# Summing the output in four column groups of TensorE instead of two, and emptying them with two copies per engine

## The chip, the cores and the metric

The kernel runs on one core of a Trainium2 chip. The metric is the device time of one execution in microseconds (us). A profile is one execution taken by the hardware profiler; its span (209.9 us for the kernel before) leaves out about 1.7 us that the timed run has (211.66 us for the same execution).

Three engines matter here: TensorE (PE in the profile, its weight loads are PEld), VectorE (DVE) and ScalarE (ACT). SPq is the queue that issues the transfers. PSUM is the memory in which TensorE's sums are kept; its rows are called partitions, and a sum lies in one of its banks. A column group is named here by the partition at which an output starts: 0, 32, 64 or 96. The granted clock (PEclk) is the share of its full speed at which TensorE runs.

## The reference, cut to what matters

One decode step of attention plus an MLP, added:

```
xn  = layernorm(x)                       # 4 x 576
A   = attention(xn, k_cache, v_cache)    # 32 heads, 16 KV heads, the last 2048 keys
A   = A.reshape(4, 4096) @ wo            # 4 x 576
B   = x1 + gelu(layernorm(x1) @ w3) @ w4 # x1 = xn + hs; one token, so hs = 0 and x1 = xn
out = x + A + B                          # 4 x 576, bfloat16
```

Some 87 MB of keys, values and weights are read for an output of 4.5 KB.

## The kernel before

All transfers are queued in one order: wq, keys and values by head, w3 and wo between them, and w4 last, in six pieces of 18, 6, 6, 4, 1 and 1 terms. A term is 128 rows of wo or w4 times 576 columns. Every term of both products, and x + xn, is added into one sum in PSUM, which is emptied at the very end.

```python
NI = 2; CW = D // NI            # two halves of 288 columns
OR = NI * B                     # 8 output rows: one for each (batch, half)
OW = OR + NI                    # weights of 4 columns, spread and padded with zeros,
ROWS = slice(NI - 1, NI - 1 + OR, NI)
gT = cleared([P, NF, OW], "gT") # so that each half lands in its own 4 of the 8 rows
op = cleared([P, WOR, OW], "op")
acc = ps_acc.tile([P, CW], F32)
nc.vector.memset(acc[:], 0.0)

def acc_matmuls(terms):         # two terms per call; late in the kernel the odd one
    for i in range(NI):         # goes to acc_odd, in another column group and bank
        for n, (lhsT, rhs) in enumerate(terms):
            to, q, start = (second[0], QD, second[1]) if second and n % 2 else (acc, 0, False)
            nc.tensor.matmul(out=to[q:q + OR, :], lhsT=lhsT[:, NI - 1 - i:NI - 1 - i + OR],
                             rhs=rhs[:, i * CW:(i + 1) * CW], start=start, stop=False, ...)
...
W4_PIECES = [0, NFH, NF - 12, NF - 6, NF - 2, NF - 1, NF]      # NF = 36
...
mlp_out(*pieces[0]); ...; mlp_out(*pieces[3])   # even terms to acc, odd terms to acc_odd
second.clear()                                  # the last two terms go to acc alone
odd = const.tile([OR, CW], F32)
nc.scalar.activation(out=odd[:], in_=acc_odd[QD:QD + OR, :], func=ACT.Copy)
seen = const.tile([1, 1], F32)
nc.vector.tensor_copy(out=seen[:], in_=odd[0:1, 0:1])
for lo, hi in pieces[4:]:
    mlp_out(lo, hi)
fin = const.tile([OR, CW], out.dtype)
nc.vector.tensor_tensor(out=fin[:], in0=acc[0:OR, :], in1=odd[:], op=ALU.add)
nc.sync.dma_start(out=o2.rearrange("b (i n) -> (b i) n", i=NI), in_=fin[:])
```

## Time and profile before

| | kernel before |
|---|---|
| median time | 211.47 us (3 runs), 211.49 us (4 runs) |
| span of the profile | 209.9 us |
| share of the span of the queue that loads | 97.5% of 16 engines |
| last w4 bytes moving | until about 206.45 us |
| store issued | 207.78 us |

The page of the kernel before: the granted TensorE clock and the DMA share in tenths, over 40 equal slices of the span, and then the line of the loading queue (packets, MB, share of the 16 engines' span).

```profile
PEclk9999769999996557976999999999997968899969
DMA  8999999999999999999999999999999999999991
...
q1 hardware_dynamic: 6640, 87.17, 97.5%
```

The transfer engines are full from the second slice to the last but one (the page has 415 GB/s read over the span). So the kernel is bound by its loads, and a change in the sum can only win in what comes after the last load. The timeline of the kernel before, at its end, shows that part (start in us, duration, engine, line, operation, output<-inputs, shape, count, and in brackets how long the engine had been idle and what ended that):

```profile
200.70 0.40 PE L183 MATMUL acc<-w_sb,gT 128*8 128x288 bf16 x1 [0.78 <-DMA w_sb<-in_B_w_dram]
200.70 0.40 PE L183 MATMUL acc_odd<-w_sb,gT 128*8 128x288 bf16 x1
200.89 0.44 PE L183 MATMUL acc<-w_sb,gT 128*8 128x288 bf16 x1
...
204.13 0.29 PE L183 MATMUL acc<-w_sb,gT 128*8 128x288 bf16 x1
...
204.25 0.29 PE L183 MATMUL acc<-w_sb,gT 128*8 128x288 bf16 x1
...
206.12 0.28 PE L183 MATMUL acc<-w_sb,gT 128*8 128x288 bf16 x1
...
206.60 0.65 PE L183 MATMUL acc<-w_sb,gT 128*8 128x288 bf16 x4
206.81 0.40 ACT L612 ACTIVATE odd<-acc_odd 8x288 f32<-8x288 f32 x1 [10.46 <-PE acc_odd L183]
207.25 0.14 DVE L614 COPY seen<-odd 1x1 f32<-1x1 f32 x1 [8.54 <-ACT odd L612]
207.32 0.43 DVE L619 TENSOR_TENSOR fin<-acc,odd 8x288 bf16<-8x288 f32 x1
207.78 0.37 SPq L620 DMA_DIRECT2D out_dram<-fin  x1
```

The two matmuls of a pair run side by side, and a pair is the work of one term. Pairs follow each other every 0.24 us at first (the granted clock is 0.50) and every 0.12 us from about 204 us on (clock 1.00). At 206.12 the piece of four terms starts; the four matmuls at 206.60 are the two last terms, one after the other in one group. The copy of acc_odd is nearly hidden behind them. Then come the add (0.43) and the store. The windows of the same stretch (busy time of each engine with its count, granted clock, DMA share, GB/s) show where the last bytes are:

```profile
206.40:206.50 0.10, 0.10 (x7) 0.07 (x3) 0.00 (x0) 0.00 (x0) 0.00 (x0) 1.00 0.08 23
206.50:206.60 0.10, 0.10 (x6) 0.07 (x1) 0.00 (x0) 0.00 (x0) 0.00 (x0) 1.00 0.00 0
```

### The profile page before, as it was taken

To read this page: it belongs to the slowest core of one execution; us is meant where nothing else is said; L and a number is where in the kernel's file an instruction comes from. 1 tells how busy PE (TensorE), PEld (TensorE's weight loads), DVE (VectorE), ACT (ScalarE), POOL (GpSimd) and SP (SyncE) were. 2 spreads that over 40 slices of the span, in tenths; PEclk is the share of its full clock that TensorE was granted. 3 is DMA by queue.
4 is the path that set the end of the run, shared out by engine and by line. 5 is a ranking of instruction groups with operands and counts; after the bars stand their busy time and mean duration, and the time that the engine had idled before them with its cause. 6 is when DMAs were issued, how large, how long until landed. Compare 5 with 4: busy or idle time off the path is not lost.

```text
span 209.9 us, 2326 instructions
## 1 busy us (share of the span) xinstructions
PE 149.1 (71%) x941; PEld 60.2 (29%) x955; DVE 113.7 (54%) x165; ACT 34.4 (16%) x66; POOL 8.9 (4%) x33
## 2 busy tenths in 40 slices
PE   0378198699670039649998999659995976898684
PEld 0123032233220013223454333224331312343353
DVE  3611877985910084917507898465949391755200
ACT  7612201021120001111120312110111111113100
POOL 4620000000000000000000300000000000000000
PEclk9999769999996557976999999999997968899969
DMA  8999999999999999999999999999999999999991
GB/s 294 406 403 440 422 428 431 437 425 432 448 429 419 421 437 421 447 418 437 434 425 437 418 426 439 434 423 440 418 431 437 422 433 431 434 428 446 417 399 71
DMA packets 6658, 87.31 MB, mean 416 GB/s; under 512 B 748, under 2 KB 1016, under 8 KB 1656
## 3 DMA queue, kind: packets, MB, share of 16 engines
q1 hardware_dynamic: 6640, 87.17, 97.5%
q8 instruction: 7, 0.11, 0.2%
q10 hardware_dynamic: 8, 0.00, 0.0%
q14 instruction: 3, 0.02, 0.0%
HBM read 87.17 MB, written 0.00 MB: 415 GB/s over the span
## 4 chain that ended last, share of the span: by engine, by line
DMA 52%; PE 24%; DVE 19%; issue 2%; ACT 1%; SPq 0%; DVEq 0%; ACTq 0%
DMA vn<-in_A_v_cache_dram 19%; DMA w_sb<-in_B_w_dram 15%; DVE kt L226 14%; DMA kn<-in_A_k_cache_dram 12%; PE S L342 9%; DMA wq_sb<-in_A_wq_dram 6%; PE acc L183 4%; PE O L394 2%; PE g_ps L460 2%; PE q_ps L286 2%; DVE mx L348 2%; PE S L364 1%; PE oT L407 1%; DVE PT L376 1%; DVE dm L350 1%
## 5 line engine op out<-in xcount | busy, mean ns | idle before, releaser
L342 PE MATMUL S<-kt,qz 128*128 128x512 bf16 x242 | 74.0, 429 | 34.5 <-DVE kt L226 31.3
L226 DVE STREAM_TRANSPOSE kt<-kn 128x2048 int32<-128x2048 int32 x32 | 73.4, 2295 | 26.5 <-DMA kn<-in_A_k_cache_dram 25.0
L342 PEld LDWEIGHTS <-qz 128*128 128x128 bf16 x256 | 24.0, 108 | 63.5 <-issue 46.6
L394 PE MATMUL O<-vn,PT 128*32 128x512 bf16 x256 | 22.9, 400 | 8.4 <-DMA vn<-in_A_v_cache_dram 8.4
L370 ACT ACTIVATE E<-S 128x512 bf16<-128x512 f32 x16 | 9.5, 597 | 97.7 <-PE S L364 97.7
L376 DVE STREAM_TRANSPOSE PT<-E 128x512 bf16<-128x512 bf16 x16 | 11.4, 710 | 15.5 <-ACT E L370 15.5
L401 ACT ACTIVATE O_sb<-O,rd 128x512 f32<-128x512 f32 x16 | 11.0, 686 | 37.1 <-PE O L394 37.1
L394 PEld LDWEIGHTS <-PT 128*32 128x32 bf16 x256 | 5.9, 94 | 29.6 <-issue 28.6
L417 DVE TENSOR_REDUCE on<-oT 128x8 bf16<-128x128 f32 x16 | 4.6, 287 | 16.7 <-PE oT L407 16.6
L348 DVE TENSOR_REDUCE mx<-S 128x1 f32<-128x512 f32 x16 | 10.5, 658 | 1.2 <-PE S L342 1.1
L407 PE MATMUL oT<-ident_w,O_sb 128*128 128x128 f32 x64 | 11.0, 296 | 0.3 <-ACT O_sb L401 0.3
L407 PEld LDWEIGHTS oT<-ident_w,O_sb 128*128 128x128 f32 x64 | 7.0, 146 | 4.6 <-issue 3.9
L183 PE MATMUL acc<-wo_sb,op 128*8 128x288 bf16 x56 | 7.5, 286 | 1.0 <-DVE op L439 1.0
L364 PE MATMUL S<-nm,j_row 8*128 8x512 bf16 x16 | 6.3, 393 | 1.9 <-DVE nm L360 1.7
L183 PE MATMUL acc<-w_sb,gT 128*8 128x288 bf16 x38 | 6.6, 342 | 0.8 <-DMA w_sb<-in_B_w_dram 0.8
L380 PE MATMUL dn<-rs,same_j 128*128 128x1 f32 x32 | 6.4, 268 | 0.0
L380 PEld LDWEIGHTS dn<-rs,same_j 128*128 128x128 f32 x32 | 5.2, 204 | 4.1 <-issue 3.4
L330 PE MATMUL S<-negbig,ohT 4*128 4x512 bf16 x16 | 6.1, 384 | 0.0
L183 PE MATMUL acc_odd<-w_sb,gT 128*8 128x288 bf16 x34 | 6.1, 350 | 0.0
L183 PEld LDWEIGHTS <-op 128*8 128x8 bf16 x64 | 4.6, 87 | 3.2 <-DVE op L439 1.1
L286 PE MATMUL q_ps<-wq_sb,xnT 128*32 128x512 bf16 x40 | 4.5, 630 | 1.3 <-DMA wq_sb<-in_A_wq_dram 1.3
L478 DVE COPY g_x<-gT_ps 128x64 f32<-128x64 f32 (+1 forms) x3 | 0.6, 194 | 8.5 <-PE gT_ps L472 8.5
(93 smaller groups left out, 80.7 us busy)
## 6 DMA issues: line engine op xcount, KB each, us to landing
kn<-in_A_k_cache_dram SPq DMA_DIRECT2D x16, 2048.0 KB, 23.8
vn<-in_A_v_cache_dram SPq DMA_DIRECT2D x16, 2048.0 KB, 25.6
wo_sb<-in_A_wo_dram SPq DMA_DIRECT2D x4, 1152.0 KB, 26.4
w_sb<-in_B_w_dram SPq DMA_DIRECT2D x1, 4608.0 KB, 33.2
wq_sb<-in_A_wq_dram SPq DMA_DIRECT2D x1, 4096.0 KB, 12.8
w_sb<-in_B_w_dram SPq DMA_DIRECT2D x1, 2592.0 KB, 32.2
w_sb<-in_B_w_dram SPq DMA_DIRECT2D x2, 864.0 KB, 34.0
w_sb<-in_B_w_dram SPq DMA_DIRECT2D x2, 576.0 KB, 32.5
```

What stands on the lines that cost most here:

```text
L183: nc.tensor.matmul(out=to[q:q + OR, :], lhsT=lhsT[:, NI - 1 - i:NI - 1 - i + OR], rhs=rhs[:, i * CW:(i + 1) * CW], start=start, stop=False ...
L226: nc.vector.transpose(out=kt[:], in_=src)
L286: nc.tensor.matmul(out=q_ps[r][g * QD:(g + 1) * QD, :], lhsT=xnT[:, k, :], rhs=wq_sb[:, col:col + NW], start=(j == 0), stop=False, skip_gr ...
L342: nc.tensor.matmul(out=S_ps[h][:], lhsT=qz[:, z0:z0 + P], rhs=kt[:, ib, c0:c0 + SC, e:2 * QD:2].rearrange("p c k -> p (c k)"), start=False ...
L348: nc.vector.reduce_max(out=mx[:], in_=S_ps[h][:], axis=AX.X)
L364: nc.tensor.matmul(out=S_ps[h][:], lhsT=j_row[:], rhs=st.pop(("nm", h))[:, 0:1].to_broadcast([NJ, NW]), start=False, stop=False, skip_grou ...
L370: nc.scalar.activation(out=E[h][:].rearrange("p c k -> p (c k)"), in_=S_ps.pop(h)[:], func=ACT.Exp, scale=scale, accum_out=rs[:])
L376: nc.vector.transpose(out=PT[h][:], in_=E.pop(h)[:])
L380: nc.tensor.matmul(out=dn[:], lhsT=same_j[:], rhs=st.pop(("rs", h))[:], start=True, stop=True)
L394: nc.tensor.matmul(out=O_ps[h][g * QD:(g + 1) * QD], lhsT=PT[h][:, c, :], rhs=vn[:, :, c, :], start=(s == 0), stop=False, skip_group_check ...
L401: nc.scalar.activation(out=O_sb[h][:], in_=O_ps.pop(h)[:], func=ACT.Copy, scale=st.pop(("rd", h))[:, 0:1])
L407: nc.tensor.transpose(out=oT[:, s, :], in_=o[:, s, :], identity=ident_w[:, s * NJ:s * NJ + P])
```

## The change

The intent: use all four column groups, so that a term takes half the streaming time; need no zero-padded weights, no second sum and no add; and empty the four quarters with two engines at once.

```diff
-    NI = 2
+    NI = 4
@@ weights and sums
-    gT = cleared([P, NF, OW], "gT")
-    op = cleared([P, WOR, OW], "op")
-    acc = ps_acc.tile([P, CW], F32)
-    nc.vector.memset(acc[:], 0.0)
+    gT = const.tile([P, NF, B], BF16, name="gT")
+    op = const.tile([P, WOR, B], BF16, name="op")
+    accs = [ps_acc.tile([P, CW], F32, name=f"acc{i}") for i in range(2)]
+    for acc in accs:
+        nc.vector.memset(acc[:], 0.0)
+    def acc_of(i):
+        return accs[i * 2 // NI][i * QD:i * QD + B, :]
@@ acc_matmuls (old body cut)
+        for lhsT, rhs in terms:
+            for i in range(NI):
+                nc.tensor.matmul(out=acc_of(i), lhsT=lhsT, rhs=rhs[:, i * CW:(i + 1) * CW],
+                                 start=False, stop=False, skip_group_check=True)
@@ mlp_g: the hidden layer gives up its own bank
-        g_ps = ps_acc.tile([P, P, n], F32, tag="g", name="g_ps")
+        g_ps = (ps_o if r < 2 else ps_m).tile([P, P, n], F32, tag="O" if r < 2 else "m", name="g_ps")
@@ the end (acc_odd, odd and seen are cut)
-    nc.vector.tensor_tensor(out=fin[:], in0=acc[0:OR, :], in1=odd[:], op=ALU.add)
-    nc.sync.dma_start(out=o2.rearrange("b (i n) -> (b i) n", i=NI), in_=fin[:])
+    fin = const.tile([B, D], out.dtype)
+    for i in range(NI):
+        dst = fin[:, i * CW:(i + 1) * CW]
+        if i * 2 < NI:
+            nc.vector.tensor_copy(out=dst, in_=acc_of(i))
+        else:
+            nc.scalar.activation(out=dst, in_=acc_of(i), func=ACT.Copy)
+    nc.sync.dma_start(out=o2, in_=fin[:])
```

Quarters 0 and 1 lie in one bank at partitions 0 and 32, quarters 2 and 3 in the other at 64 and 96. VectorE empties the first bank, ScalarE the second.

More of the change, by code (lines that the diff above doesn't have):

```diff
@@ L166 @@
     qz = cleared([P, ZP + Hkv * 4 * P], "qz")
-    OR = NI * B
-    OW = OR + NI
-    ROWS = slice(NI - 1, NI - 1 + OR, NI)
-    gT = cleared([P, NF, OW], "gT")
-    op = cleared([P, WOR, OW], "op")
-    acc = ps_acc.tile([P, CW], F32)
-    nc.vector.memset(acc[:], 0.0)
-    second = []
-    def acc_matmuls(terms):
-        for i in range(NI):
-            for n, (lhsT, rhs) in enumerate(terms):
-                to, q, start = (second[0], QD, second[1]) if second and n % 2 else (acc, 0, False)
-                nc.tensor.matmul(out=to[q:q + OR, :], lhsT=lhsT[:, NI - 1 - i:NI - 1 - i + OR],
-                                 rhs=rhs[:, i * CW:(i + 1) * CW], start=start, stop=False, skip_group_check=True)
-                if start:
-                    second[1] = False
+    gT = const.tile([P, NF, B], BF16, name="gT")
[5 more added lines that the diff above has]
+        return accs[i * 2 // NI][i * QD:i * QD + B, :]
+    def acc_matmuls(terms):
+        for lhsT, rhs in terms:
+            for i in range(NI):
+                nc.tensor.matmul(out=acc_of(i), lhsT=lhsT, rhs=rhs[:, i * CW:(i + 1) * CW],
+                                 start=False, stop=False, skip_group_check=True)
     def layernorm(dst_f, dst_bf, src):
@@ L268 @@
     nc.vector.reduce_sum(out=own[:], in_=ident_f[:].rearrange("p (h d) -> p h d", h=WOH), axis=AX.X)
-    idz = const.tile([B, OW], F32)
-    nc.gpsimd.memset(idz[:], 0.0)
-    nc.gpsimd.tensor_copy(out=idz[:, ROWS], in_=ident_f[0:B, 0:B])
     xsum = xn_f
     nc.gpsimd.tensor_tensor(out=xsum[:], in0=xn_f[:], in1=x_bf[:], op=ALU.add)
-    acc_matmuls([(idz[:], xsum)])
+    acc_matmuls([(ident_f[0:B, 0:B], xsum)])
     ln2_bf = part(D, B)
@@ L438, in o_pick @@
         with nc.allow_low_precision("one term is not zero"):
-            nc.vector.reduce_sum(out=op[:, :, ROWS], in_=mk[:].rearrange("p i h b -> p i b h"), axis=AX.X)
+            nc.vector.reduce_sum(out=op[:], in_=mk[:].rearrange("p i h b -> p i b h"), axis=AX.X)
     def o_proj(h):
@@ L443, in o_proj @@
             return
-        for i in range(0, WOR, 2):
-            acc_matmuls([(op[:, i + u, :], wo_tiles[h // WOQ][:, i + u, :]) for u in range(2)])
+        acc_matmuls([(op[:, i, :], wo_tiles[h // WOQ][:, i, :]) for i in range(WOR)])
     G_CHUNKS = [(e, 4 * g, 4) for e in range(2) for g in range(NQD)] + [(e, 16, 2) for e in range(2)]
@@ L486, in mlp_act @@
         nc.gpsimd.tensor_scalar(out=u[:], in0=u[:], scalar1=0.5, scalar2=0.5, op0=ALU.mult, op1=ALU.add)
-        nc.gpsimd.tensor_tensor(out=gT[:, :, ROWS], in0=u[:], in1=xs[:], op=ALU.mult)
+        nc.gpsimd.tensor_tensor(out=gT[:], in0=u[:], in1=xs[:], op=ALU.mult)
     def mlp_out(lo, hi):
         w4 = w_tiles["w4"]
-        for i in range(lo, hi, 2):
-            acc_matmuls([(gT[:, u, :], w4[:, u, :]) for u in range(i, min(i + 2, hi))])
+        acc_matmuls([(gT[:, u, :], w4[:, u, :]) for u in range(lo, hi)])
     order = [("K", 0), ("K", 1), ("K", 2)]
@@ L598 @@
     pieces = list(zip(W4_PIECES, W4_PIECES[1:]))
-    acc_odd = ps_acc.tile([P, CW], F32, tag="g", name="acc_odd")
-    second += [acc_odd, True]
     o_turn(hl)
@@ L605 @@
     o_proj(hl)
-    mlp_out(*pieces[0])
-    mlp_out(*pieces[1])
-    mlp_out(*pieces[2])
-    mlp_out(*pieces[3])
-    second.clear()
-    odd = const.tile([OR, CW], F32)
-    nc.scalar.activation(out=odd[:], in_=acc_odd[QD:QD + OR, :], func=ACT.Copy)
-    seen = const.tile([1, 1], F32)
-    nc.vector.tensor_copy(out=seen[:], in_=odd[0:1, 0:1])
-    for lo, hi in pieces[4:]:
-        mlp_out(lo, hi)
-    fin = const.tile([OR, CW], out.dtype)
-    nc.vector.tensor_tensor(out=fin[:], in0=acc[0:OR, :], in1=odd[:], op=ALU.add)
-    nc.sync.dma_start(out=o2.rearrange("b (i n) -> (b i) n", i=NI), in_=fin[:])
+    for lo, hi in pieces:
+        mlp_out(lo, hi)
+    fin = const.tile([B, D], out.dtype)
[6 more added lines that the diff above has]
+    nc.sync.dma_start(out=o2, in_=fin[:])
 _INS = ['A_x', 'A_k_cache', 'A_v_cache', 'A_wq', 'A_wo', 'B_x', 'B_w1', 'B_w2', 'B_w3', 'B_w4']
```

## The prediction

> What bounds it now. The transfers. The 40-slice rows show DMA at 9 or more in every slice but the first and last, and the queue table gives the loading queue 97.5% of the span; in the chain of waits DMA holds 52%. Windows of the end: the last w4 bytes move until about 206.45 us of the 209.9 us span. So the change can only win in what lies after that, 3.45 us, of which the store (issue at 207.78 to the end) is 2.1.
>
> The end before (timeline, chain): the first half of w4 lands at 200.65; then matmul pairs (acc and acc_odd, 288 columns, side by side, one pair is one term's work) run one every 0.24 us while the granted clock is 0.50 (to 203.8), then every 0.12 us at 1.00. PE lags the data until 205.97, takes the piece of four terms at 206.12 and the two one-term pieces from 206.60 to 207.25. The copy of acc_odd (ScalarE 0.40) and the one-element copy (0.14) are hidden or nearly so; the add into fin takes 0.43 (207.32 to 207.75).
>
> What the change does there. A term becomes 4 weight loads and 4 matmuls of 144 columns in four column groups. If the four run side by side, streaming halves: estimated 0.12 us per term at clock 0.50, 0.06 at 1.00. But issue may bind: the R group (8 loads, 8 matmuls of 32 columns in 0.35 us with its latency) gives an estimate of 25 to 30 ns per load-matmul pair, 0.11 us per term. [...] So about 0.11 instead of 0.12 at full clock, 0.13 instead of 0.24 at half. PE then catches up with the data by about 203 and idles between pieces. [...] So PE may stay at half clock, and the last six terms cost about 0.8 us from 206.1: last matmul end 206.9 to 207.2, against 207.25.
>
> Evacuation: odd, seen and the add go; two copies of 4x144 on each engine come. VectorE's add of 288 took 0.43; a copy of 144 is estimated at 0.28, two overlapped 0.49. ScalarE: 4x128 took 0.27, 8x288 0.40, so two about 0.47, in parallel. That is 0.06 MORE than the add. The store (4 rows of 1152 bytes for 8 of 576) stays about 2.1.
>
> Off the path: clearing gT and op (ScalarE 0.33+0.22), idz, the middle projections; g_ps now shares the O and m buffers, which may hold PE for under 1 us near 100 to 112 us, where loads are queued 24 us ahead (DMA table): nothing reaches the end.
>
> Sum: 0.05 to 0.4 us gained after the last byte, less 0.06: about 0.2. Predicted 211.25 us, range 210.7 to 211.7. Chances: faster by over 2% 0.01, within 2% 0.98, slower by over 2% 0.01.
>
> What would show it: loading queue still 97%, last w4 bytes at 206.2 to 206.7; PE idle between w4 pieces; 110 to 130 ns per term; VectorE's two fin copies about 0.49; last byte to end 3.0 to 3.4 us.
>
> What would make it wrong: the four groups not overlapping (0.24 us per term or more at full clock, PE ends at about 209); a stall near 100 to 112 us that starves the queue; weight loads that don't hide; a store of 4 rows that is quicker or slower.

The 0.11 us per term rests on the R group alone (8 matmuls in 0.35 us; the trace of the kernel before has them 25 ns apart from the second on). That TensorE may stay at half clock was the estimate: in the kernel before the granted clock was 0.50 from 200.58 us to 204.00 and 1.00 from there to the store.

## The result, and the profile after

The changed kernel took 211.73 us (median of 4 runs, 211.45 to 212.0), the kernel before 211.49 us (4 runs, 211.39 to 211.6). The ratio is 1.0011, 95% interval 0.9994 to 1.0029: no difference that these runs can tell from zero. A ratio here and below is the mean time of one kernel's fast runs over that of the other's of the same rounds, so it is not quite the ratio of the medians. The predicted 0.2 us gain did not appear, and 211.73 lies just above the predicted range of 210.7 to 211.7.

The page after, loading queue:

```profile
q1 hardware_dynamic: 6632, 87.17, 97.5%
```

The timeline of the changed kernel at its end:

```profile
200.76 1.30 PE L181 MATMUL acc<-w_sb,gT 128*4 128x144 bf16 x72
...
202.83 0.55 PE L181 MATMUL acc<-w_sb,gT 128*4 128x144 bf16 x24 [0.78 <-DMA w_sb<-in_B_w_dram]
...
204.96 0.89 PE L181 MATMUL acc<-w_sb,gT 128*4 128x144 bf16 x24 [1.58 <-DMA w_sb<-in_B_w_dram]
...
206.35 1.01 PE L181 MATMUL acc<-w_sb,gT 128*4 128x144 bf16 x24 [0.51 <-DMA w_sb<-in_B_w_dram]
...
207.40 0.61 DVE L602 CAST fin<-acc 4x144 bf16<-4x144 f32 x2 [7.38 <-PE acc L181]
207.44 0.58 ACT L604 ACTIVATE fin<-acc 4x144 bf16<-4x144 f32 x2 [10.01 <-PE acc L181]
208.09 0.34 SPq L605 DMA_DIRECT2D out_dram<-fin  x1
```

Much went as predicted: TensorE has caught up with the loads and waits for each piece. The four groups do run side by side: the first 18 terms are 72 matmuls in 1.30 us. Less some 0.23 us of latency of the last ones (four matmuls alone take 0.23 us in after_onecopy), that is 1.07 us over 71 starts, 15 ns each in the mean, so 0.06 us per term; the prediction had 0.11. (One by one, the trace has the four matmuls of a term start 3 to 5 ns apart, and the next term 0.06 us later.) The windows of the same kernel show the clock at the end, and its last bytes about 0.3 us later than in the profile before:

```profile
204.00:205.00 1.00, 0.04 (x4) 0.04 (x7) 0.00 (x0) 0.00 (x0) 0.00 (x0) 0.91 0.97 371
205.00:206.00 1.00, 0.85 (x24) 0.64 (x24) 0.00 (x0) 0.00 (x0) 0.00 (x0) 0.50 0.59 213
...
206.60:206.80 0.20, 0.20 (x19) 0.20 (x9) 0.00 (x0) 0.00 (x0) 0.00 (x0) 0.50 0.09 29
206.80:207.00 0.20, 0.20 (x12) 0.12 (x4) 0.00 (x0) 0.00 (x0) 0.00 (x0) 0.50 0.00 0
```

So there are three suspects: the copies (0.61 us for two, with nothing overlapped, where the add took 0.43), the half clock in the last six terms, and loads that end later. The chain of waits of the changed kernel has all three in a row, the landing of the four-term piece at 206.31, TensorE's last 1.06 us and the copies (start, us, what; steps of 0.04 us and less are left out):

```profile
175.19 31.13 DMA w_sb<-in_B_w_dram
...
206.35 1.06 PE acc L181 x23
...
207.44 0.28 ACT fin L604
207.72 0.29 ACTq L631
```

The last line is the second ScalarE copy: the profile calls its wait for the first one "ACTq".

To compare profiles whose loads end at different moments, three moments of each timeline are used below: the first matmul of the four-term piece (A), the start of the first instruction that empties the final sum (B), and the issue of the store (C). A to B is TensorE and the last two pieces, B to C is the emptying, C to the end of the span is the store. For the kernel before A is 206.12, B is 207.32, C is 207.78 and the end 209.9; for the changed one 206.35, 207.40, 208.09 and 210.2. So A to B shrank from 1.20 to 1.05, B to C grew from 0.46 to 0.69, and the store stayed at 2.1.

A to B still holds the wait for the last two pieces. So a fourth moment stands beside them, L, when the last piece has landed. It is read from the completions of transfers in the trace, which the views shown here do not print: 206.81 before, 207.03 after.

### The profile page after: what moved, and what is told of

Same layout as the page of the kernel before. It is cut to its first block, busy times and chain, and to the rows that moved or that the text cites. A ratio compares the mean times of both kernels' runs of the same rounds, so it can differ in the third digit from the quotient of the medians.

```text
span 210.2 us, 2618 instructions
## 1 busy us (share of the span) xinstructions
PE 145.4 (69%) x1095; PEld 57.3 (27%) x1095; DVE 114.0 (54%) x166; ACT 34.2 (16%) x65; POOL 8.7 (4%) x31
## 3 DMA queue, kind: packets, MB, share of 16 engines
q1 hardware_dynamic: 6632, 87.17, 97.5%
## 4 chain that ended last, share of the span: by engine, by line
DMA 74%; PE 16%; DVE 7%; ACT 1%; issue 0%; SPq 0%; ACTq 0%; DVEq 0%
DMA kn<-in_A_k_cache_dram 31%; DMA vn<-in_A_v_cache_dram 23%; DMA w_sb<-in_B_w_dram 15%; DMA wq_sb<-in_A_wq_dram 6%; PE S L335 5%; DVE kt L222 5%; PE O L387 2%; PE g_ps L452 2%; PE q_ps L279 2%; PE acc L181 1%; PE oT L400 1%; PE gT_ps L464 1%; DVE qz L311 1%; PE dn L373 1%; PE S L357 1%; ACT q_sb L290 1%
## 5 line engine op out<-in xcount | busy, mean ns | idle before, releaser
L335 PE MATMUL S<-kt,qz 128*128 128x512 bf16 x256 | 77.2, 430 | 31.1 <-DVE kt L222 30.9
L387 PE MATMUL O<-vn,PT 128*32 128x512 bf16 x256 | 24.1, 420 | 12.0 <-DMA vn<-in_A_v_cache_dram 12.0
L400 PE MATMUL oT<-ident_w,O_sb 128*128 128x128 f32 x64 | 12.7, 335 | 0.0
L400 PEld LDWEIGHTS oT<-ident_w,O_sb 128*128 128x128 f32 x64 | 8.4, 168 | 5.0 <-issue 4.3
L279 PE MATMUL q_ps<-wq_sb,xnT 128*32 128x512 bf16 x40 | 3.9, 564 | 2.9 <-DMA wq_sb<-in_A_wq_dram 2.9
L181 PE MATMUL acc<-w_sb,gT 128*4 128x144 bf16 x144 | 3.7, 255 | 2.9 <-DMA w_sb<-in_B_w_dram 2.9
L602 DVE CAST fin<-acc 4x144 bf16<-4x144 f32 x2 | 0.6, 297 | 7.4 <-PE acc L181 7.4
L452 PE MATMUL g_ps<-w_sb,ln2T 128*32 128x512 bf16 (+1 forms) x50 | 4.5, 443 | 0.0
```

The lines of the kernel that those rows point to most:

```text
L279: nc.tensor.matmul(out=q_ps[r][g * QD:(g + 1) * QD, :], lhsT=xnT[:, k, :], rhs=wq_sb[:, col:col + NW], start=(j == 0), stop=False, skip_gr ...
L335: nc.tensor.matmul(out=S_ps[h][:], lhsT=qz[:, z0:z0 + P], rhs=kt[:, ib, c0:c0 + SC, e:2 * QD:2].rearrange("p c k -> p (c k)"), start=False ...
L387: nc.tensor.matmul(out=O_ps[h][g * QD:(g + 1) * QD], lhsT=PT[h][:, c, :], rhs=vn[:, :, c, :], start=(s == 0), stop=False, skip_group_check ...
L400: nc.tensor.transpose(out=oT[:, s, :], in_=o[:, s, :], identity=ident_w[:, s * NJ:s * NJ + P])
L452: nc.tensor.matmul(out=g_ps[g * QD:(g + 1) * QD], lhsT=ln2T[:, k, :], rhs=rhs, start=(j == 0), stop=False, skip_group_check=True)
```

## The experiments

Theory 1: nothing but the end of the kernel counts; what TensorE gained there the two copies per engine took back, and the later loads of the profile are chance. Theory 2: the change makes the loads end later, for example because the hidden layer's sum moved to shared buffers. Inside theory 1 the half clock competed with the copies.

### The two kernels again (before_again, after_again, before_third, after_third)

No edit. They give the spread.

> The kernel before, unchanged, as a control: how far the last w4 byte and the time move from run to run. Both theories: ratio 1.000 within 0.002. Theory 1 (the end of the kernel decides; the 0.3 us by which the last byte came later with the change is chance): the last w4 byte lies anywhere from 206.4 to 206.8 us, as in the changed kernel. Theory 2 (the change lengthens the stream of loads): it lies at 206.4 to 206.5 again, and only here.

> The changed kernel, unchanged. Theory 1: ratio 0.999 to 1.001; from the last byte to the end again 3.4 to 3.5 us, last byte 206.4 to 206.8. Theory 2: the last byte again at 206.7 or later, ratio 1.001 to 1.002.

> The kernel before, for its last-piece times in one more profile: four-term piece to store issue 1.65 to 1.75 us, ratio 1.000 within 0.0013.

> The changed kernel again, on the same chip as packed_again. Four-term piece to store issue 1.77 us as twice before (before: 1.65 to 1.71), so ratio to before 1.000 to 1.001.

| profile | A | A to B | B to C | C to end | L | L to B | L to end | time, median us | ratio to before (95%) |
|---|---|---|---|---|---|---|---|---|---|
| before | 206.12 | 1.20 | 0.46 | 2.1 | 206.81 | 0.51 | 3.08 | 211.49 | |
| before_again | 206.04 | 1.20 | 0.47 | 2.1 | 206.71 | 0.53 | 3.08 | 211.57 | 1.0000 (0.9988 to 1.0012) |
| before_third | 205.93 | 1.20 | 0.46 | 2.1 | 206.61 | 0.52 | 3.09 | 211.72 | 1.0004 (0.9990 to 1.0018) |
| after | 206.35 | 1.05 | 0.69 | 2.1 | 207.03 | 0.37 | 3.19 | 211.73 | 1.0011 (0.9994 to 1.0029) |
| after_again | 206.03 | 1.03 | 0.69 | 2.1 | 206.70 | 0.36 | 3.19 | 211.66 | 1.0004 (0.9991 to 1.0017) |
| after_third | 206.25 | 0.93 | 0.69 | 2.1 | 206.79 | 0.39 | 3.21 | 211.76 | 1.0009 (0.9996 to 1.0023) |

The emptying is the same to 0.01 us every time, and 0.23 us longer with the change. Measured from A, TensorE's part is 0.15 to 0.27 us shorter, 0.20 in the mean, and the whole part after A differs by 0.03 us. But in after_third the last piece landed 0.58 us after the four-term one, where the other five profiles have 0.71 to 0.74, and this alone shortens its A to B (and made its expectation of 1.77 us to the store issue miss: 1.66 from the landing of the four-term piece). Measured from L, the profiles of each kernel agree to 0.03 us: TensorE gains 0.15 us, the emptying loses 0.23, and L to the end is 0.11 us longer with the change. More than the gain is given back.

A itself moves by 0.2 to 0.3 us from run to run of one kernel. That spread is not made at the end: the time at which VectorE gets one key tile that it has waited for early in the run was 74.08, 74.21 and 74.38 us in three profiles of the kernel before, and 73.99, 74.22 and 74.57 us in three of the changed kernel. Theory 2's own mark (the last byte at 206.7 or later again) did not come: in after_again A was back at 206.03. A's mean is still 0.18 us later with the change (206.21 against 206.03, three profiles each) and L's 0.13 (206.84 against 206.71); but five other profiles with the sums of the change (after_onecopy, after_dve4, after_same, halves and wide, below) have L at 206.71 in the mean too, which speaks for chance. All three ratios lie above 1, though each interval holds 1. Taken together, the 14 runs of the changed kernel have a mean of 211.73 us and the 24 runs of the kernel before in the same rounds 211.57; of these 0.16 us, 0.11 lie after L. Whether the other 0.05 belong to the change stays open.

### Only the move of the hidden layer's sum (before_gps)

The kernel before with this one line of the change:

```diff
-        g_ps = ps_acc.tile([P, P, n], F32, tag="g", name="g_ps")
+        g_ps = (ps_o if r < 2 else ps_m).tile([P, P, n], F32, tag="O" if r < 2 else "m", name="g_ps")
```

> The kernel before with only the move of g_ps into the O and m buffers. Both theories of the end: no change (ratio 1.000 within 0.0012), last w4 piece as before. If the move holds up the loads: last piece 0.2 us or more later, ratio above 1.0012.

Ratio 1.0001 (0.9989 to 1.0014), A at 205.97, A to B 1.19, B to C 0.47. The move costs nothing that reaches the end, as predicted, and this version of theory 2 falls.

### Keeping TensorE's clock up (after_warm)

```diff
+    idle = ps_s.tile([P, NW], F32, tag="S", name="idle")
+    def keep_busy(n):
+        for _ in range(n):
+            nc.tensor.matmul(out=idle[:], lhsT=ident_bf[:], rhs=qz[:, 0:NW], start=True, stop=True)
-    for lo, hi in pieces:
+    for k, (lo, hi) in enumerate(pieces):
+        keep_busy({1: 3, 2: 7, 3: 4}.get(k, 0))
         mlp_out(lo, hi)
```

> The changed kernel with idle matmuls of 512 columns (3, 7 and 4, into a bank that nobody reads) between the w4 pieces. Theory 1 (half clock costs about 0.4 us in the last six terms): granted clock 1.00 to the end, the last 24 matmuls in 0.5 to 0.6 us instead of 1.01, time 0.3 to 0.45 us under the changed kernel (ratio about 0.998 of it). If the clock at the end does not matter: same time as the changed kernel within 0.1 us.

It lost: ratio 1.0046 (1.0015 to 1.0077), with times from 211.5 to 213.93 us. The timeline of this kernel:

```profile
200.43 2.33 PE L181 MATMUL acc<-w_sb,gT 128*4 128x144 bf16 x72 [1.10 <-DMA w_sb<-in_B_w_dram]
...
202.69 1.02 PE L593 MATMUL idle<-qz,ident_bf 128*128 128x512 bf16 x3
...
204.12 1.69 PE L593 MATMUL idle<-qz,ident_bf 128*128 128x512 bf16 x7
...
206.21 1.04 PE L593 MATMUL idle<-qz,ident_bf 128*128 128x512 bf16 x4
...
207.18 0.55 PE L181 MATMUL acc<-w_sb,gT 128*4 128x144 bf16 x24
```

In this run the clock was already at 0.50 when w4 came, the first 72 matmuls took 2.33 us, and the idle matmuls, counted for a full clock, stood in front of the real ones. At full clock and with all data there, the last 24 matmuls do take 0.55 us and not 1.01. Whether that would help is answered by runs made for other reasons: the last six terms of after_onecopy, after_dve4 and wide (below) ran at a granted clock of 1.00, and their A to B is 1.04, 1.02 and 0.99, no less than the 1.05, 1.03 and 0.93 of the changed kernel at half clock. The timeline of after_onecopy, and a window of it with the clock, show why:

```profile
206.05 0.61 PE L183 MATMUL acc<-w_sb,gT 128*4 128x144 bf16 x20 [0.83 <-DMA w_sb<-in_B_w_dram]
206.83 0.23 PE L183 MATMUL acc<-w_sb,gT 128*4 128x144 bf16 x4 [0.17 <-DMA w_sb<-in_B_w_dram]
...
206.40:206.50 0.10, 0.10 (x10) 0.08 (x4) 0.00 (x0) 0.00 (x0) 0.00 (x0) 1.00 0.01 0
```

A faster TensorE is through with five terms early and then waits (0.17 us here) for the last piece, which lands some 0.75 us after the four-term one. The half clock fits into that time, and up to L it costs nothing. After L it costs a little: L to B is 0.31 to 0.32 us in these three profiles and 0.36 to 0.39 in those of the changed kernel, so about 0.05 us.

### One copy per engine (after_onecopy), and all four on VectorE (after_dve4)

The first leaves out quarters 1 and 3 (they are zero in the output); the second doubles the suspected cost:

```diff
 # after_onecopy (fin is cleared at the start)
     for i in range(NI):
+        if i % 2:
+            continue
 # after_dve4
-        if i * 2 < NI:
+        if True:
             nc.vector.tensor_copy(out=dst, in_=acc_of(i))
```

> Wrong result on purpose: each engine copies only its first quarter, so half of the output is zero. Theory 1 (the second copy of each engine is fully on the path): 0.3 us under the changed kernel, the gap from last matmul to store issue 0.35 instead of 0.68 us. If the copies overlap or hide, 0.1 us or less. Theory 2 says nothing of it.

> The changed kernel with all four quarter copies on VectorE: the suspected cost doubled. Theory 1 (each copy of 4x144 takes its full 0.30 us on the path): the emptying 1.2 instead of 0.61 us, time 0.6 us over the changed kernel, ratio to before 1.003. If copies overlap: less than 0.3 us over it.

The timelines, first of after_onecopy, then of after_dve4:

```profile
207.09 0.30 DVE L605 CAST fin<-acc 4x144 bf16<-4x144 f32 x1 [7.04 <-PE acc L183]
207.14 0.28 ACT L607 ACTIVATE fin<-acc 4x144 bf16<-4x144 f32 x1 [9.93 <-PE acc L183]
207.47 0.34 SPq L608 DMA_DIRECT2D out_dram<-fin  x1
```

```profile
207.13 1.25 DVE L602 CAST fin<-acc 4x144 bf16<-4x144 f32 x4 [7.08 <-PE acc L181]
208.40 0.35 SPq L605 DMA_DIRECT2D out_dram<-fin  x1
```

B to C is 0.38 us with one copy per engine, 0.69 with two and 1.27 with four on one engine: each further copy in a row costs about 0.3 us, all of it on the path. The times go the same way: after_onecopy 211.47 us (ratio 0.9997, 0.9985 to 1.0009), after_dve4 212.31 us (1.0038, 1.0025 to 1.0051). Of these two only the second interval lies clear of 1; after_onecopy is 0.19 us under after_again, where 0.3 was expected, and their intervals overlap. In the profiles, the second copy of each engine is what took the gain back.

### Why two copies do not overlap (after_same, packed_two)

The prediction had subtracted an overlap, as other pairs show it (two copies of 0.19 us in 0.29 us, early in the kernel). In after_same each engine reads its first quarter twice, so size, count and target stay and only the rows of the source change. Its output is wrong, which doesn't matter for the time.

```diff
-            nc.vector.tensor_copy(out=dst, in_=acc_of(i))
+            nc.vector.tensor_copy(out=dst, in_=acc_of(i // 2 * 2))
```

with the same edit for ScalarE. packed_two cuts the single copy of the packed kernel (below) into two over neighbouring columns of the same rows.

> Wrong result on purpose: each engine's second copy reads the same four rows again instead of the rows of the next column group, 32 partitions further. Size, count and target stay. If the two copies did not overlap because the source rows change: now 0.54 us for two on VectorE, 0.50 on ScalarE. If a copy out of the sums never overlaps the next: 0.61 and 0.58 as before.

> The packed kernel with each engine's one copy of 8x144 cut into two of 8x72. A copy costs about 0.15 us of its own and 1 ns a column (estimated from 0.30 for 144 and 0.45 for 288 columns), so 0.22 us each. If the count of copies is what costs: 0.44 us for two (0.37 if they overlap) instead of 0.30, for the same number of columns.

Timelines of after_same and of packed_two:

```profile
207.08 0.51 DVE L602 CAST fin<-acc 4x144 bf16<-4x144 f32 x2 [8.46 <-PE acc L181]
207.12 0.46 ACT L604 ACTIVATE fin<-acc 4x144 bf16<-4x144 f32 x2 [10.86 <-PE acc L181]
```

```profile
207.08 0.36 DVE L613 CAST fin<-acc 8x72 bf16<-8x72 f32 x2 [8.07 <-PE acc L188]
207.12 0.33 ACT L614 ACTIVATE fin<-acc 8x72 bf16<-8x72 f32 x2 [10.95 <-PE acc L188]
```

With the same source rows two copies take 0.51 and 0.46 us instead of 0.61 and 0.58, so they take about 0.1 us less on both engines and overlap. In packed_two two copies of 0.22 us take 0.36. The overlap is lost when the second copy reads rows 32 partitions further on. Neither program has a wait between the two copies, so it is nothing that the program orders. Each is one look, but both engines of both kernels agree. What inside the engines does it is not shown.

### Halves instead of quarters (halves)

```diff
-    NI = 4
+    NI = 2
```

Two column groups, one copy of 4x288 per engine.

> The changed kernel with two halves of 288 columns in two column groups, instead of four quarters: one copy of 4x288 per engine. Theory 1: copies 0.43 instead of 0.61 us, landing to store issue about 0.82 us, time 0.1 to 0.25 us under before. If the number of copies does not matter: as the changed kernel.

Ratio 1.0001 (0.9988 to 1.0013). B to C is 0.52 us (the copy takes 0.45), A to B 1.05, together 1.57 against 1.66 of before and 1.62 to 1.74 in the three profiles of the change. L to the end is 3.03 us against 3.08 of before: a gain of 0.05 us in one profile, too small for the times, whose expected gain of 0.1 to 0.25 did not show.

### One copy per engine and one store (packed, packed_again)

The kernel before, keeping its padded weights (8 rows for batch and half), but with quarters in two groups, so that a bank is emptied by one copy of 8x144 (the hidden layer's sum moves as in the change):

```diff
+                for f in range(NG2):
+                    lo = i * CW + f * QW
+                    nc.tensor.matmul(out=acc_of(f), lhsT=lhsT[:, NI - 1 - i:NI - 1 - i + OR],
+                                     rhs=rhs[:, lo:lo + QW], start=False, stop=False, skip_group_check=True)
...
+    nc.vector.tensor_copy(out=fin[:, 0:QW], in_=acc_of(0))
+    nc.scalar.activation(out=fin[:, QW:CW], in_=acc_of(1), func=ACT.Copy)
```

> The before kernel's zero-padded weights kept (8 rows, one for each batch and half), but column quarters in two column groups and two banks, so that one copy of 8x144 per engine empties everything. Theory 1 (after the last w4 piece lands, only the last term's matmuls and the emptying count): landing to store issue about 0.7 us (0.29 matmuls, 0.30 copies, two hand-overs) against 0.98 of before and 1.05 of the change; time 0.2 to 0.35 us under before, ratio 0.9985 to 0.999. Rival (the load stream is longer with the sum in separate groups): no gain over before.

> The same kernel as the run packed, once more, beside the changed kernel on one chip, since its first interval still held 1. If the gain seen inside the profile (four-term piece to store issue 1.36 us against 1.70 of before) is real: 0.1 to 0.35 us under before again, and 0.2 to 0.5 us under the changed kernel. If the first run was luck: within 0.1 us of before.

Timelines of packed and of packed_again (that one as it stands from 203 us on), and a window of the second:

```profile
206.38 0.92 PE L188 MATMUL acc<-w_sb,gT 128*8 128x144 bf16 x24 [0.59 <-DMA w_sb<-in_B_w_dram]
...
207.32 0.30 DVE L611 CAST fin<-acc 8x144 bf16<-8x144 f32 x1 [8.48 <-PE acc L188]
...
207.70 0.37 SPq L613 DMA_DIRECT2D out_dram<-fin  x1
```

```profile
202.70 4.97 PE L188 MATMUL acc<-w_sb,gT 128*8 128x144 bf16 x132
...
207.70 0.29 DVE L611 CAST fin<-acc 8x144 bf16<-8x144 f32 x1 [7.66 <-PE acc L188]
...
204.00:205.00 1.00, 1.00 (x34) 1.00 (x32) 0.00 (x0) 0.00 (x0) 0.00 (x0) 0.95 0.92 357
```

The first run had a full clock and gained: L to C 0.77 us, where about 0.7 was expected, against 0.97 to 0.99 of before. Its ratio was 0.9992 (0.9978 to 1.0005). The second gave 1.0004 (0.9991 to 1.0016), so the gain did not repeat in the times. Its profile, the slowest of its five runs (211.96 us, median 211.49), had the clock at half until about 204.1 (the last line gives 0.95 for 204 to 205), and here, where a term took 0.24 us at half clock (the first three of w4 took 0.72 us), TensorE never caught up: there is no wait between pieces, and it ended 0.4 us later. The half clock, which cost the four-group kernel about 0.05 us, held this two-group one back much more. That the clock made the difference between the two runs rests on one profile each.

### Four groups and one copy per engine (wide)

The copy covers 36 partitions, which takes both groups of a bank at once (the rows between are zeros); the result lies in two row ranges and needs two stores:

```diff
# acc_of (cut): quarters 0 and 2 now lie in the first bank, 1 and 3 in the second
+    fin = const.tile([QD + B, 2 * CW], out.dtype)
+    nc.vector.tensor_copy(out=fin[:, 0:CW], in_=accs[0][0:QD + B, :])
+    nc.scalar.activation(out=fin[:, CW:], in_=accs[1][2 * QD:3 * QD + B, :], func=ACT.Copy)
+    nc.sync.dma_start(out=o2[:, 0:2 * CW], in_=fin[0:B, :])
+    nc.scalar.dma_start(out=o2[:, 2 * CW:], in_=fin[QD:QD + B, :])
```

> The changed kernel with its four column groups kept, but one copy per engine over 36 partitions that takes both of its groups, then two stores of 4 rows on two queues. If the emptying (two copies that do not overlap, 0.61 us and hand-overs) is what ate the gain: emptying 0.30 us, four-term piece to store issue about 1.45 us against 1.70 of before and 1.77 of the change; time 0.1 to 0.3 us under before, ratio 0.9985 to 0.9995, and no runs that PE holds up late. If a copy over 36 partitions costs more than one over 4, or the second store ends later: no gain over before.

```profile
205.96 0.95 PE L182 MATMUL acc<-w_sb,gT 128*4 128x144 bf16 x24 [0.85 <-DMA w_sb<-in_B_w_dram]
...
206.95 0.30 DVE L600 CAST fin<-acc 36x144 bf16<-36x144 f32 x1 [7.08 <-PE acc L182]
206.98 0.29 ACT L601 ACTIVATE fin<-acc 36x144 bf16<-36x144 f32 x1 [9.95 <-PE acc L182]
207.33 0.27 ACTq L603 DMA_DIRECT2D out_dram<-fin  x1
207.33 0.34 SPq L602 DMA_DIRECT2D out_dram<-fin  x1
```

A copy over 36 partitions costs what one over 4 does (0.30 us), and the stores are issued 1.37 us after A, against 1.66 of before. The predicted gain is there up to this point, 0.3 us of it. But from the issue to the end of the span it took 2.3 us instead of 2.1, so with the pair of stores most of it is given back: L to the end is 3.03 us against 3.08. The ratio is 1.0001 (0.9988 to 1.0013), so the second of the two ways to fail came true. No kernel of this study is clearly faster than the kernel before.

## Why the prediction was wrong

- That the loads bind and only some 3.4 us at the end can be won: right. The loading queue holds 97.5% in both kernels, and, the misplaced idle matmuls apart, everything that was changed at the end moved the time by 0.8 us or less.
- That TensorE would catch up and idle between the pieces: right; it waited 0.78, 1.58 and 0.51 us.
- That issue binds at 0.11 us per term: wrong. It was 0.06 us, half of the 0.12 us that a pair of 288 columns takes at full clock in the kernel before. The prediction took its 25 to 30 ns per matmul from the R group, whose matmuls, with 128x128 weights, start 25 ns apart in the trace. With 128x4 weights in four column groups the trace has 15 ns in the mean, 3 to 5 ns within a term, so the estimate did not carry over. What sets either spacing is not shown. It made no difference to the end, since TensorE waits for data.
- That the last six terms run at half clock and end 0.05 to 0.35 us earlier than before: right in size (A to B is 0.15 to 0.27 us shorter, L to B 0.15) and in the clock (0.50), though the half clock cost only about 0.05 us: three kernels whose last terms ran at full clock have about the same A to B, since there the last piece, landing about 0.75 us after the four-term one, sets the end. What moves the clock is not shown. In the changed kernel it fell from 1.00 to 0.50 in gaps without matmuls of 2.08 us (at about 194.6) and of 1.58 us (at about 204.8). The length of one gap does not decide it: in after_again a gap of 1.57 us left it at 1.00, and in the next, of 0.85 us, it fell to 0.50.
- **The step that failed is the emptying: "That is 0.06 MORE than the add."** The mechanism was named, its size was off by a factor of four. From its start to the store issue the emptying takes 0.69 us instead of 0.46: 0.23 us more. The two copies were expected to overlap and take 0.49; they took 0.61, because the second reads rows 32 partitions away (after_same, one look). That is 0.18 of the 0.23; the rest is in the hand-over, where ScalarE starts 0.04 us after VectorE and the store waits for both.
- The sum: after L, 0.15 us gained on TensorE less 0.23 lost in the emptying, and 0.03 more to the end of the span, is a loss of 0.11 us where a gain of 0.2 was predicted. The rest of the measured +0.24 us of medians (+0.10 and +0.20 in the two repetitions, 0.16 in the mean of all runs) is in when the loads end, which moves by 0.2 to 0.3 us between runs of one kernel; whether the change has a small part in it is open. The range ended 0.2 us above the time before and left too little room for that spread.
- Two engines emptying at once, as in the change, was not enough; one copy per engine that takes both groups of a bank (wide) brings the emptying from 0.69 to 0.38 us.

## What to carry to other kernels

When a sum is split over more column groups, count the instructions that empty it, at their full cost each (here 0.30 us for 144 columns and 0.45 for 288 on VectorE; an estimate from these two is that about half of the 0.30 is fixed), and lay the groups out so that one instruction per engine reads them all into rows that one store can take. No kernel here shows a gain from that in its time, only in its profile. In this kernel, bound by its loads, a faster engine at the end only waited for the last piece (0.17 us in after_onecopy); what follows the last landing in series (the last term, copies, hand-overs, the store: 3.08 to 3.09 us from L to the end before, 3.19 to 3.21 with the change) is all that could be won. A forecast of tenths of a microsecond needs a range as wide as the spread of the load stream, and profiles are best compared from the landing of the last load, not from the start of the span and not from an earlier piece.
